# Attention: the out-projection directly behind P·V, its maximum pairs at other places, tile 14's maxima rounded in two halves

## Chip, cores and metric

The kernel runs on one core of a Trainium2 chip. The metric is device time in microseconds (us) of that core, lower is better. A step of the profile is read by the engines' short names: PE is TensorE (PEld its weight loads), DVE VectorE, ACT ScalarE, POOL GpSimd, SP SyncE.

## The reference

The program is two rounds of a Fourier layer and an attention layer with one shared K/V head, each with a residual, on x of shape 1 x 2048 x 512. There are 32 heads of width 16.

```python
x = x + _A_ref(_layernorm(x), ...)     # y = Cr@a - Ci@b,  a, b = x @ Wd_re.T, x @ Wd_im.T
x = x + _B_ref(_layernorm(x), wq, wk, wv, wo)
# the same two lines once more

def _B_ref(x, wq, wk, wv, wo):
    q = heads(x @ wq);  k = x @ wk;  v = x @ wv
    scores = jnp.einsum("bhqd,bkd->bhqk", q, k) * (Dh ** -0.5)
    p = _softmax(scores, axis=-1)
    o = jnp.einsum("bhqk,bkd->bhqd", p, v)
    return merge_heads(o) @ wo
```

The change touches only the attention layer (`_B_ref`), which runs twice, as layer 0 and layer 1.

## The kernel before

Each layer has a phase A (Fourier layer, Q, K, V) and a phase B (attention). Phase B goes through 16 query tiles of 128 rows. A tile `i` takes 32 steps `s_`: two halves of the heads by 16 key blocks of 128 keys. The order of all instructions is written by hand; each engine runs its own in that order and waits on semaphores.

In a step of `phase_b` TensorE does three things. First `pv` (L787): P·V of the step two before, eight matmul passes that write columns of bank `z`. Then `score` (L773): four score matmuls, 64 rows deep, so that two run beside each other in the two halves of the array; two of them fill a `pair()` of banks `x`, of which there are two, and ScalarE takes the exponential of a pair at once (L776). Between the scores stand up to three maxima: `max_half` (L350) computes the scores of a later tile against 512 keys into one of three banks `y`, and VectorE reduces them to a maximum per row (L351). These maxima are needed before a tile's own scores, since the softmax subtracts them: `max_neg` negates and rounds them into a high and a low part, and `max_rows` transposes them (L379), copies them (L381) and sends them by four DMAs of SyncE into the rows of the query tile that the score matmul adds. For most tiles this is done at steps 27 and 29 of the tile before. For tile 0 and tile 15 it is done in two halves: the first there (for tile 0 ahead of attention), the second at steps 11 and 13 of the tile itself.

The maxima are a list `units`, in order of tile, head pair, key quarter and half `g`. `owed(n)` lets three go in a step, after a lead of 12 ahead of attention, and `more_max` takes the next. The head pair has two maxima, one for each half of the array; when both are issued together they run side by side (a pair of maxima, below).

The tile's result goes out in the steps of the next tile (`out_tasks`): store, sums, reciprocal and load in steps 1 to 6, scaling (L827) and splitting (L833, L834) on GpSimd in steps 9 and 10. At the end of step 12 stands `o_proj`: twelve full-size matmuls (L86 to L88) that accumulate into one bank `y`, with a pair of maxima behind the sixth and the twelfth; `o_add` (L852) adds the residual on VectorE and issues the DMA of the result (L853), on GpSimd's queue in layer 0 and SyncE's in layer 1. So the projection of tile `i - 1` stands in the steps of tile `i`; 14 tiles of each layer (0 to 13) have pairs in it, tile 14's stands where no maxima are left, and tile 15's is done behind the steps.

Once all maxima are done, in tile 15, the last two scores of a step go to banks `y` of their own (L766), each with its own exponential (L768).

Of the kernel before, what the change touches and what calls it, by code (L numbers as in the profile page):

```python
# [17 lines left out]
P = 128  # L18
# [22 lines left out]
KEPT = [e for e in EARLY if e[0]]  # L41
QSLOT = (8, 0, 1, "h", "l", 8, 0, 1, "h", "l", 8, 0, 1, 8, 0, 1)
HALF = NPAIR // 2


@with_exitstack
def fnet_mqa_kernel(ctx: ExitStack, tc: tile.TileContext, x_in, ct, dt_, wq, wkv, wo, out):
# [50 lines left out]
    nc.gpsimd.memset(v1[:, :, DH:DH + 1], 1.0)  # L98
    kone = sb.tile([P, 1], F32, name="kone")
    kmask = sb.tile([P, 1], F32, name="kmask")  # L100
    t_ = sb.tile([P, 1], F32, name="ktmp")
    nc.vector.tensor_reduce(kone[:64], ident[:64, M0:M0 + 2], op=ALU.add, axis=AX.X)
    nc.vector.tensor_reduce(kone[64:], ident[64:, 64 + M0:64 + M0 + 2], op=ALU.add, axis=AX.X)
    nc.vector.tensor_reduce(t_[:64], ident[:64, M0:64], op=ALU.add, axis=AX.X)
# [82 lines left out]
    def make_layer(L, src, mid, dst, last):  # L187
# [176 lines left out]
        def max_neg(i, p0=0, n=NPAIR, k=4):  # L364
            nm = sb.tile([P, NPAIR, 2], F32, name="nm")[:, :n, :]
            nc.vector.tensor_reduce(nm, o.mxp[i][:, p0:p0 + n, :, :k], op=ALU.max, axis=AX.X, negate=True)
            if p0 + n == NPAIR:
                o.mxp.pop(i)
            nmv = nm.rearrange("p a g -> p g a")
            ms = sb.tile([P, 2, 2, NPAIR], F32, name="ms").rearrange("p g r a -> p (g r a)")  # L370
            ms = ms[:, :4 * n].rearrange("p (g r a) -> p g r a", g=2, r=2)
            nc.vector.tensor_copy(ms[:, :, 0, :].bitcast(F32R), nmv)
            nc.vector.tensor_sub(ms[:, :, 1, :].bitcast(F32R), nmv, ms[:, :, 0, :])
            st["ms"] = ms
# [160 lines left out]
        def phase_a(extra):  # L535
# [193 lines left out]
                if g == 0:  # L729
                    v_tr(12, 4, vt[0])  # L730
            max_neg(0, 0, HALF, 5)
            for k in range(12):
                more_max()
                if k == 2:
                    max_rows(0, 0, HALF, nc.scalar)

        early = {e[:2] for e in EARLY}
        units = [(0, pr, g, 3) for pr in range(HALF, NPAIR) for g in range(2)]
        units += [(i, pr, g, kb) for i in range(1, NT) for pr in range(NPAIR) for kb in range(4) for g in range(2)
                  if (i, kb) not in early]  # L740
        o.done = o.extra = 0

        def more_max():
            if o.done < len(units) and units[o.done][0] in o.loaded | {0}:
                max_half(*units[o.done])
                o.done += 1

        def owed(n):
            return min(3 * (n + 1) + 12 + o.extra, len(units)) - o.done

        def done_with(i, pr):
            return all(u[:2] > (i, pr) for u in units[o.done:])

        ptiles = {}

        def score(i, s_, j):
            hf, c = divmod(s_, NT)
            jj, g = divmod(j, 2)
            cp = 4 * (2 * hf + jj)
            if (i, s_) not in ptiles:  # L760
                k = i * NSTEP + s_
                ptiles[i, s_] = slot((6, 7, 2)[k % 3]).rearrange("p (j n) -> p j n", j=4)
            w = j // 2
            if i == NT - 1 and jj == 1 and o.done == len(units):
                e = bank("y")
                nc.tensor.matmul(e, kz[64 * g:64 * g + KR, c * P:(c + 1) * P],  # L766
                                 o.qT[i][64 * g:64 * g + KR, cp:cp + 4, :], start=True, stop=True)
                nc.scalar.activation(ptiles[i, s_][:, j, :], e, AF.Exp, scale=DH ** -0.5)  # L768
                return
            first = "e" not in st  # L770
            if first:
                st["e"] = pair()
            nc.tensor.matmul(st["e"][:, g, :], kz[64 * g:64 * g + KR, c * P:(c + 1) * P],  # L773
                             o.qT[i][64 * g:64 * g + KR, cp:cp + 4, :], start=True, stop=True)
            if not first:
                nc.scalar.activation(ptiles[i, s_][:, 2 * w:2 * w + 2, :], st.pop("e"), AF.Exp, scale=DH ** -0.5)  # L776
# [48 lines left out]
        def o_scale(i, hf):  # L825
            cs = slice(hf * 256, hf * 256 + 256)
            nc.gpsimd.tensor_mul(bt["ot"][:, cs], bt["ot"][:, cs], bt["den"][:, cs])  # L827
# [14 lines left out]
        def o_proj(i):  # L842
            for k in range(NK):
                o_mm(k)
                if k % 2 and i < NT - 1:
                    for _ in range(2):
                        more_max()
                        o.extra += 1
            o_add(i)

        def o_add(i):
            nc.vector.tensor_add(bt["x"], bt["po"], bt["x"])  # L852
            (nc.sync if last else nc.gpsimd).dma_start(dst[i], bt["x"])  # L853

        def finish():
            i = NT - 1
            oa = acc.pop((i, 1))
            x_load(i)
            pt = bank("y")
            for b in range(4):  # L860
                nc.tensor.transpose(pt[:, b * P:(b + 1) * P], oa[:, b * P:(b + 1) * P], ident)
            o_mm(0)
            o_mm(1)
            p4 = pt.rearrange("p (b j r) -> p b j r", b=4, j=4)
            rc = sb.tile([P, 4, 4], F32, name="rc")
            nc.vector.reciprocal(rc, p4[:, :, :, DH])
            on = half(5)[:, :256]
            for jj in range(2):
                nc.vector.tensor_tensor(
                    on[:, jj * P:(jj + 1) * P].rearrange("p (b g d) -> p b g d", b=4, g=2),  # L870
                    p4[:, :, 2 * jj:2 * jj + 2, :DH],
                    rc[:, :, 2 * jj:2 * jj + 2].unsqueeze(3).to_broadcast([P, 4, 2, DH]), op=ALU.mult)
            pt = bank("y")[:, :256]
            for jj in range(2):
                nc.tensor.transpose(pt[:, jj * P:(jj + 1) * P], on[:, jj * P:(jj + 1) * P], ident)
            split_ps(pt, bt["oh"][:, 256:], bt["ol"][:, 256:])
            o_mm(2)
            o_mm(3)
            o_add(i)

        o.finish = finish

# [25 lines left out]
        def phase_b(nxt):  # L908
# [10 lines left out]
            for n in range(NT * NSTEP):  # L919
                i, s_ = divmod(n, NSTEP)  # L920
                if len(behind) == 2:
                    pv(*behind.pop(0))
                behind.append((i, s_))
                g = units[o.done][2] if o.done < len(units) else 1
                for j, m in ((1 - g, 1), (g, 2), (3 - g, 0), (2 + g, 1)):
                    score(i, s_, j)
                    for _ in range(m):
                        if owed(n) >= 1:
                            more_max()
                if i == 0 and 2 <= s_ <= 8 and s_ % 2 == 0:  # L930
                    q_half_store(14, s_ // 2 - 1)
                if n == 12:
                    osp = slot(3, F32R).rearrange("p (a h n) -> p a h n", a=2, h=2)
                if i == 0 and s_ in (12, 14, 16, 18):
                    j = s_ // 2 - 6
                    split_sb(st["wo", j], woh[:, j, :], wol[:, j, :], nc.gpsimd)
                if i > 0:
                    for fn in out_tasks(i - 1).get(s_, ()):
                        fn()
                if s_ == 2:  # L940
                    for j in range(2, NT):
                        if i == max(0, j - 4 if j < 13 else j - 2):
                            qT_load(j)
                for fn in half_tasks(i).get(s_, ()):
                    fn()
                for at, j, p0, np_ in ((NT - AHEAD, i, HALF, HALF), (NSTEP - AHEAD, i + 1, 0, HALF if i == NT - 2 else NPAIR)):
                    if j in (0, NT - 1) or j == i + 1 < NT:
                        if s_ == at:
                            assert done_with(j, p0 + np_ - 1)
                            max_neg(j, p0, np_)  # L950
                        if s_ == at + 2:
                            max_rows(j, p0, np_)
# [6 lines left out]
        def half_tasks(i):  # L959
            return {  # L960
                18: [lambda: o_store(i, 0)], 19: [lambda: o_sum(i, 0)], 22: [lambda: o_inv(i, 0)],
                23: [lambda: o_load(i, 0)], 27: [lambda: o_scale(i, 0)], 29: [lambda: o_hi(i, 0)],
            }

        def out_tasks(i):
            return {
                1: [lambda: o_store(i, 1), lambda: o_sum(i, 1), lambda: x_load(i)], 5: [lambda: o_inv(i, 1)],
                6: [lambda: o_load(i, 1)], 9: [lambda: o_scale(i, 1)], 10: [lambda: o_hi(i, 1)],
                12: [lambda: o_proj(i)], 14: [lambda: o_stats(i)], 16: [lambda: o_rstd(i)],
                25: [lambda: o_ln(i)], 26: [lambda: o_xnh(i)], 27: [lambda: o_xnl(i)],  # L970
            }

        woh = wol = osp = None
# [48 lines left out]
```

## Time and profile before

| | us |
|---|---|
| three runs: median (lowest to highest) | 3716.96 (3715.03 to 3717.65) |
| the profiled execution: its time | 3724.12 |
| its span, first to last instruction | 3722.3 |
| attention of layer 0, about | 690 to 1865 |
| attention of layer 1, about | 2541 to 3713 |

The times of attention are those of the first and last P·V matmuls in the trace. The granted TensorE clock is 1.00 in attention and 0.99 over the span. In the views a row of the timeline gives the start (us from the span's start), the duration, the engine, the line, the operation with its output and inputs, the number of instructions merged, and in brackets the idle time before them with the releaser. Two rows of one engine can overlap, since matmuls and vector operations are pipelined.

### The profile page before, as it was taken

What the parts mean: (1) busy time and instruction counts of PE and PEld (TensorE: products, weight loads), DVE (VectorE), ACT (ScalarE), POOL (GpSimd) and SP (SyncE); (2) the same over time, 40 slices, a digit from 0 to 9 for tenths busy, and PEclk for the clock granted to TensorE, in tenths of its full rate; (3) what the DMA queues carried; (4) which work ended last, traced back from release to release, by engine and by line L of the source; (5) the groups of instructions that cost most, each with busy time, mean ns of one, the idle gap of its engine ahead of it and who ended that gap; (6) DMA issues with size and microseconds to landing.
All of it is one profiled execution on the core that took longest, in us unless ns stands there. A gap on an engine that the chain in (4) does not pass through costs nothing. (4 is left out here: it accounts for less than half of the span.)

```text
span 3722.3 us, 64512 instructions
## 1 busy us (share of the span) xinstructions
PE 3631.1 (98%) x25474; PEld 1909.3 (51%) x25474; DVE 2798.4 (75%) x4767; ACT 2400.3 (64%) x3104; POOL 777.3 (21%) x984
## 2 busy tenths in 40 slices
PE   8999999999999999999999999999999999999999
PEld 6786768533433333334377766684343334333333
DVE  5167978788888888888311779778888888888882
ACT  4322222688888888888933231227888888888888
POOL 5534332111111111111154342421000000000000
PEclk9999999999999999999999999999999999999999
DMA  5444241311111100110143342313111111001100
GB/s 176 133 136 125 97 119 52 101 32 50 33 36 31 49 22 24 33 47 23 40 131 104 129 124 92 110 64 89 47 33 36 33 49 34 22 22 50 33 24 25
DMA packets 204736, 243.00 MB, mean 65 GB/s; under 512 B 36880, under 2 KB 160784, under 8 KB 197264
## 3 DMA queue, kind: packets, MB, share of 16 engines
q1 hardware_dynamic: 199504, 222.08, 20.1%
q0 software_dynamic: 4864, 16.78, 1.5%
q8 instruction: 199, 3.26, 0.4%
q14 instruction: 105, 0.86, 0.1%
q10 hardware_dynamic: 64, 0.02, 0.0%
HBM read 174.58 MB, written 63.17 MB: 64 GB/s over the span
## 5 line engine op out<-in xcount | busy, mean ns | idle before, releaser
L776 ACT ACTIVATE slot<-x 128x1024 f32<-128x1024 f32 x1990 | 1943.1, 1027 | 334.4 <-PE x L773 265.5
L351 DVE TENSOR_REDUCE mxp<-y 128x1 f32<-128x512 f32 x3040 | 1908.1, 684 | 281.5 <-PE y L350 233.3
L787 PE MATMUL z<-slot,v 128*32 128x512 f32 x8192 | 1096.3, 605 | 1.9 <-ACT row L790 1.9
L773 PE MATMUL x<-slot,kz 64*128 64x512 f32 x2956 | 900.9, 447 | 3.6 <-DMA slot<-mt 3.5
L773 PEld LDWEIGHTS x<-slot,kz 64*128 64x128 f32 x2956 | 375.3, 185 | 731.5 <-ACT slot L776 598.5
L350 PE MATMUL y<-kz,slot 64*128 64x512 f32 x2208 | 726.2, 435 | 4.8 <-ACT mt L381 0.7
L338 DVE TENSOR_REDUCE mxe<-y 128x1 f32<-128x512 f32 x832 | 516.4, 682 | 189.4 <-PE y L336 184.7
L660 PE MATMUL x<-ch,xnh 64*128 64x512 f32 (+1 forms) x2048 | 507.8, 390 | 16.3 <-DVE slot L74 8.9
L660 PE MATMUL x<-ch,xnl 64*128 64x512 f32 (+1 forms) x2048 | 475.2, 369 | 0.0
L660 PE MATMUL x<-cl,xnh 64*128 64x512 f32 (+1 forms) x2048 | 474.7, 369 | 0.0
L350 PEld LDWEIGHTS y<-kz,slot 64*128 64x128 f32 x2208 | 349.5, 185 | 94.5 <-DVE mxp L351 27.5
L827 POOL TENSOR_TENSOR row<-row,row 128x256 f32<-128x256 f32 x63 | 46.3, 735 | 1677.8 <-DMA row<-rd 1422.6
L336 PE MATMUL y<-kz,slot 64*128 64x512 f32 (+1 forms) x1088 | 354.3, 420 | 33.7 <-DVE mxe L338 20.7
L78 POOL TENSOR_TENSOR cl<-craw,ch 128x512 fp32r<-128x512 f32 x236 | 303.1, 1303 | 289.2 <-ACT ch L77 229.3
L787 PEld LDWEIGHTS z<-slot,v 128*32 128x32 f32 x8192 | 163.6, 108 | 277.3 <-issue 249.2
L660 PEld LDWEIGHTS x<-ch,xnh 64*128 64x128 f32 x2048 | 268.7, 189 | 69.2 <-issue 16.4
L660 PEld LDWEIGHTS x<-ch,xnl 64*128 64x128 f32 x2048 | 280.7, 189 | 33.3
L660 PEld LDWEIGHTS x<-cl,xnh 64*128 64x128 f32 x2048 | 281.7, 190 | 28.0
L77 ACT CAST ch<-craw 128x512 fp32r<-128x512 f32 x256 | 154.8, 620 | 161.8 <-PE x L660 89.5
L666 ACT COPY junk<-x 128x2 f32<-128x2 f32 x256 | 40.5, 158 | 332.3 <-PE x L660 253.6
L336 PEld LDWEIGHTS y<-kz,slot 64*128 64x128 f32 x1088 | 171.8, 188 | 129.4 <-DVE mxe L338 90.5
L338 DVE TENSOR_REDUCE mxp<-y 128x1 f32<-128x512 f32 (+1 forms) x256 | 144.4, 617 | 24.7 <-PE y L336 21.5
(148 smaller groups left out, 3141.7 us busy)
## 6 DMA issues: line engine op xcount, KB each, us to landing
craw<-ct_in SPq DMA_DIRECT2D x112, 512.0 KB
slot<-qd SPq DMA_DIRECT2D x44, 1024.0 KB
qd<-row SPq DMA_DIRECT2D x144, 128.0 KB
od<-row SPq DMA_DIRECT2D x252, 64.0 KB
row<-x_in SPq DMA_DIRECT2D x32, 256.0 KB
mid<-row POOLq DMA_DIRECT2D x32, 256.0 KB, 2.4
craw<-ct_in SPq DMA_DIRECT2D x32, 256.0 KB
row<-mid SPq DMA_DIRECT2D x32, 256.0 KB
```

The lines of the kernel that those rows point to most:

```text
L77: nc.scalar.copy(hi, raw)
L78: (eng or nc.vector).tensor_sub(lo, raw, f(hi))
L336: nc.tensor.matmul(pm[g], o.qT[i][gs, pr, :], kz[gs, c0:c0 + n], start=True, stop=True)
L338: nc.vector.reduce_max(to[:, g:g + 1], pm[g], axis=AX.X)
L350: nc.tensor.matmul(pm, o.qT[i][gs, pr, :], kz[gs, kb * 512:kb * 512 + 512], start=True, stop=True)
L351: nc.vector.reduce_max(partial(i)[:, pr, g, kb:kb + 1], pm, axis=AX.X)
L660: nc.tensor.matmul(z[d][:, cols], w, hl[j][t == 1][rs_], start=m == 0 and ph == 0 and j == t == 0, stop=j == 1 and t == 2 and (ph == 0 or ...
L666: nc.scalar.copy(junk, zp[dd][:, :, cols.start])
L773: nc.tensor.matmul(st["e"][:, g, :], kz[64 * g:64 * g + KR, c * P:(c + 1) * P], o.qT[i][64 * g:64 * g + KR, cp:cp + 4, :], start=True, sto ...
L776: nc.scalar.activation(ptiles[i, s_][:, 2 * w:2 * w + 2, :], st.pop("e"), AF.Exp, scale=DH ** -0.5)
L787: nc.tensor.matmul(a[32 * j:32 * j + 32, :], v1[:, c, :], pt[:, j, :], start=c == 0, stop=c == NT - 1)
L827: nc.gpsimd.tensor_mul(bt["ot"][:, cs], bt["ot"][:, cs], bt["den"][:, cs])
```

## The change

Five things change in phase B; nothing else does, apart from two small tiles that are dropped (`ms` and `ktmp` use other buffers).

- `o_proj(i - 1)` stands directly behind the P·V of step 12, ahead of that step's scores, not at the step's end.
- Its pairs of maxima stand behind the third and the ninth matmul, and for tiles 9 to 13 also behind the sixth.
- Step 11 has two maxima (no `odd` one). All other steps have two of one pair (`whole`) and one half of another (`odd`), whose other half is taken in the next step.
- Tile 14 is rounded in two halves, as tile 15 is: `HALVED`.
- The DMA of the result is issued by SyncE in both layers, in step 13 (`o_out`); scaling and splitting on GpSimd stand together in steps 28 and 10.

```diff
+HALVED = (0, NT - 2, NT - 1)
...
-            ms = sb.tile([P, 2, 2, NPAIR], F32, name="ms").rearrange("p g r a -> p (g r a)")
-            ms = ms[:, :4 * n].rearrange("p (g r a) -> p g r a", g=2, r=2)
+            ms = half(0 if i or p0 else 2)[:, :4 * n].rearrange("p (g r a) -> p g r a", g=2, r=2)
...
-            for k in range(12):
-                more_max()
-                if k == 2:
+            for k in range(6):
+                max_both(*pick_pair(0))
+                if k == 1:
                     max_rows(0, 0, HALF, nc.scalar)
...
+        def pick_odd(n):
+            if "odd" in st:
+                return *st.pop("odd"), 1
+            pick = pick_pair(n, n + 1)
+            if pick:
+                st["odd"] = pick
+                return *pick, 0
+            return None
+
+        def max_both(j, pr, kb):
+            for g in range(2):
+                max_half(j, pr, g, kb)
...
         def o_proj(i):
             for k in range(NK):
                 o_mm(k)
-                if k % 2 and i < NT - 1:
-                    for _ in range(2):
-                        more_max()
-                        o.extra += 1
+                if (k in (0, 2) or k == 1 and 8 < i) and i < NT - 1:
+                    pick = pick_pair(NSTEP * (i + 1) + 12)
+                    if pick:
+                        max_both(*pick)
             o_add(i)
...
-            (nc.sync if last else nc.gpsimd).dma_start(dst[i], bt["x"])
+
+        def o_out(i):
+            nc.sync.dma_start(dst[i], bt["x"])
...
                 behind.append((i, s_))
-                g = units[o.done][2] if o.done < len(units) else 1
-                for j, m in ((1 - g, 1), (g, 2), (3 - g, 0), (2 + g, 1)):
-                    score(i, s_, j)
-                    for _ in range(m):
-                        if owed(n) >= 1:
-                            more_max()
+                if i > 0 and s_ == 12:
+                    o_proj(i - 1)
+                whole = pick_pair(n)
+                odd = pick_odd(n) if i == 0 or s_ != 11 else None
+                g = odd[3] if odd else 1
+                score(i, s_, 1 - g)
+                if whole:
+                    max_half(*whole[:2], g, whole[2])
+                score(i, s_, g)
+                if whole:
+                    max_half(*whole[:2], 1 - g, whole[2])
+                if odd:
+                    max_half(*odd[:2], g, odd[2])
+                score(i, s_, 3 - g)
+                score(i, s_, 2 + g)
...
-                    if j in (0, NT - 1) or j == i + 1 < NT:
+                    if j in HALVED or j == i + 1 < NT:
...
-                23: [lambda: o_load(i, 0)], 27: [lambda: o_scale(i, 0)], 29: [lambda: o_hi(i, 0)],
+                23: [lambda: o_load(i, 0)], 28: [lambda: o_scale(i, 0), lambda: o_hi(i, 0)],
...
-                6: [lambda: o_load(i, 1)], 9: [lambda: o_scale(i, 1)], 10: [lambda: o_hi(i, 1)],
-                12: [lambda: o_proj(i)], 14: [lambda: o_stats(i)], 16: [lambda: o_rstd(i)],
+                6: [lambda: o_load(i, 1)], 10: [lambda: o_scale(i, 1), lambda: o_hi(i, 1)],
+                12: [lambda: o_proj(i)] if i == NT - 1 else [],
+                13: [lambda: o_out(i)], 14: [lambda: o_stats(i)], 16: [lambda: o_rstd(i)],
```

`pick_pair` takes the next head pair and key quarter whose query tile is loaded, in the same order as `units` had them. The lines of the code shift: P·V is L815 after, the scores L801, the maxima L351 with their reduction in L352, the projection L87 to L89, the addition L880.

What TensorE has in step 12 of tile 4 in layer 0, from its last two scores to the P·V of step 13 (`slot_9653` is the query tile of the maxima, `slot_8282` the weights of the projection), before:

```order
L773 MATMUL x<-xnl,kz 128x512 x2
L86 MATMUL y<-slot_7957,slot_8282 128x512
L87 MATMUL y<-slot_7958,slot_8282 128x512
L88 MATMUL y<-slot_7957,slot_8282 128x512
L86 MATMUL y<-slot_7957,slot_8282 128x512
L87 MATMUL y<-slot_7958,slot_8282 128x512
L88 MATMUL y<-slot_7957,slot_8282 128x512
L350 MATMUL y<-kz,slot_9653 128x512 x2
```

The same six matmuls and one more pair follow, and then P·V. After, from the P·V of step 12 on:

```order
L815 MATMUL z<-slot_11449,v_74 32x512 x4
L87 MATMUL y<-slot_7956,slot_8281 128x512
L88 MATMUL y<-slot_7957,slot_8281 128x512
L89 MATMUL y<-slot_7956,slot_8281 128x512
L351 MATMUL y<-kz,slot_9649 128x512 x2
```

and at the end of the same projection, with the scores and maxima of step 12 behind it:

```order
L351 MATMUL y<-kz,slot_9649 128x512 x2
L87 MATMUL y<-slot_7956,slot_8281 128x512
L88 MATMUL y<-slot_7957,slot_8281 128x512
L89 MATMUL y<-slot_7956,slot_8281 128x512
L801 MATMUL x<-xnl,kz 128x512
L351 MATMUL y<-kz,slot_9649 128x512
L801 MATMUL x<-xnl,kz 128x512
L351 MATMUL y<-kz,slot_9649 128x512 x2
L801 MATMUL x<-xnl,kz 128x512 x2
```

The scores have moved from ahead of the projection to behind it, and its last pair has moved from its end to three matmuls ahead of its end; the bank of the projection is now asked for again by the third maximum of the same step.

The projection of tile 9 (step 12 of tile 10, layer 0), after, from its first to its third pair:

```order
L351 MATMUL y<-kz,slot_14540 128x512 x2
L87 MATMUL y<-slot_7956,slot_8281 128x512
L88 MATMUL y<-slot_7957,slot_8281 128x512
L89 MATMUL y<-slot_7956,slot_8281 128x512
L351 MATMUL y<-kz,slot_14540 128x512 x2
L87 MATMUL y<-slot_7956,slot_8281 128x512
L88 MATMUL y<-slot_7957,slot_8281 128x512
L89 MATMUL y<-slot_7956,slot_8281 128x512
L351 MATMUL y<-kz,slot_14540 128x512 x2
```

Here a pair stands behind every third matmul; before, the two pairs of every projection were six matmuls apart.

The last maxima, in tile 15 of either layer, stand in step 3 before and in steps 3, 4 and (one of them) 5 after.

More of the change, by code (lines that the diff above doesn't have):

```diff
@@ L100, in fnet_mqa_kernel @@
     kmask = sb.tile([P, 1], F32, name="kmask")
-    t_ = sb.tile([P, 1], F32, name="ktmp")
+    t_ = junk[:, :1]
     nc.vector.tensor_reduce(kone[:64], ident[:64, M0:M0 + 2], op=ALU.add, axis=AX.X)
@@ L731, in phase_a @@
             max_neg(0, 0, HALF, 5)
-            for k in range(12):
-                more_max()
-                if k == 2:
+            for k in range(6):
+                max_both(*pick_pair(0))
+                if k == 1:
                     max_rows(0, 0, HALF, nc.scalar)
         early = {e[:2] for e in EARLY}
-        units = [(0, pr, g, 3) for pr in range(HALF, NPAIR) for g in range(2)]
-        units += [(i, pr, g, kb) for i in range(1, NT) for pr in range(NPAIR) for kb in range(4) for g in range(2)
-                  if (i, kb) not in early]
@@ L741, in make_layer @@
[L741 to L749, printed above, removed]
-        def done_with(i, pr):
-            return all(u[:2] > (i, pr) for u in units[o.done:])
+        groups = {}
+        for i in range(NT):
+            for hf in range(2) if i in HALVED else (None,):
+                prs = range(NPAIR) if hf is None else range(HALF * hf, HALF * hf + HALF)
+                if i or hf:
+                    kbs = [kb for kb in range(4) if (i, kb) not in early] if i else [3]
+                    at = NSTEP * i + NT - AHEAD if hf else NSTEP * (i - 1) + NSTEP - AHEAD
+                    groups[i, hf] = {"at": at, "whole": [(pr, kb) for pr in prs for kb in kbs]}
@@ new lines, in in_reach, with pick_pair @@
+        def in_reach(j, n):
+            return j in o.loaded | {0} and (j <= 1 or n >= NSTEP * max(0, j - 4 if j < 13 else j - 2) + 8)
+        def pick_pair(n, until=0):
+            for (j, _), g in groups.items():
+                if not in_reach(j, n):
+                    return None
+                if g["at"] < until:
+                    continue
+                if g["whole"]:
+                    pr, kb = g["whole"].pop(0)
+                    return j, pr, kb
+            return None
@@ new lines, in pick_odd @@
+        def pick_odd(n):
[5 more added lines that the diff above has]
+                return *pick, 0
+            return None
+        def max_both(j, pr, kb):
+            for g in range(2):
+                max_half(j, pr, g, kb)
+        def done_with(i, pr):
+            if "odd" in st and st["odd"][0] <= i and st["odd"][1] <= pr:
+                return False
+            return not any(q <= pr for (j, _), g in groups.items() if j <= i for q, *_ in g["whole"])
@@ L754, in make_layer, with all_done @@
+        def all_done():
+            return not any(g["whole"] for g in groups.values()) and "odd" not in st
         ptiles = {}
@@ L763, in score @@
             w = j // 2
-            if i == NT - 1 and jj == 1 and o.done == len(units):
+            if i == NT - 1 and jj == 1 and all_done():
                 e = bank("y")
@@ L879, in finish @@
             o_add(i)
+            o_out(i)
         o.finish = finish
@@ L945, in phase_b @@
                     fn()
-                for at, j, p0, np_ in ((NT - AHEAD, i, HALF, HALF), (NSTEP - AHEAD, i + 1, 0, HALF if i == NT - 2 else NPAIR)):
-                    if j in (0, NT - 1) or j == i + 1 < NT:
+                for at, j, p0, np_ in ((NT - AHEAD, i, HALF, HALF),
+                                       (NSTEP - AHEAD, i + 1, 0, HALF if i + 1 in HALVED else NPAIR)):
+                    if j in HALVED or j == i + 1 < NT:
                         if s_ == at:
-                            assert done_with(j, p0 + np_ - 1)
+                            assert done_with(j, p0 + np_ - 1), (n, j, p0, groups)
                             max_neg(j, p0, np_)
@@ L967, in out_tasks @@
                 1: [lambda: o_store(i, 1), lambda: o_sum(i, 1), lambda: x_load(i)], 5: [lambda: o_inv(i, 1)],
-                6: [lambda: o_load(i, 1)], 9: [lambda: o_scale(i, 1)], 10: [lambda: o_hi(i, 1)],
-                12: [lambda: o_proj(i)], 14: [lambda: o_stats(i)], 16: [lambda: o_rstd(i)],
-                25: [lambda: o_ln(i)], 26: [lambda: o_xnh(i)], 27: [lambda: o_xnl(i)],
+                6: [lambda: o_load(i, 1)], 10: [lambda: o_scale(i, 1), lambda: o_hi(i, 1)],
+                12: [lambda: o_proj(i)] if i == NT - 1 else [],
+                13: [lambda: o_out(i)], 14: [lambda: o_stats(i)], 16: [lambda: o_rstd(i)],
+                25: [lambda: o_ln(i), lambda: o_xnh(i)], 26: [lambda: o_xnl(i)],
             }
```

## The prediction

> **What bounds the kernel now.** I read the busy shares first, then a window that holds only attention (its columns are TensorE, its weight loads, VectorE, ScalarE and GpSimd), then the timeline of single steps.
>
> ```profile
> PE 3631.1 (98%) x25474; PEld 1909.3 (51%) x25474; DVE 2798.4 (75%) x4767; ACT 2400.3 (64%) x3104; POOL 777.3 (21%) x984
> ```
>
> ```profile
> 800.00:1800.00 1000.00, 993.50 (x6730) 392.96 (x6722) 880.80 (x1505) 855.72 (x910) 147.65 (x312) 1.00 0.12 33
> ```
>
> The averages say TensorE (98%), and inside attention TensorE has 99%, VectorE 88% and ScalarE 86% (880.80 and 855.72 us of 1000). A matmul counts as busy while it drains, so 99% does not show that TensorE sets the pace. For that one ordinary step is read: TensorE, then the sum of its weight loads' waits for a score bank (us, times, longest), then ScalarE.
>
> ```profile
> 1006.06 1.07 PE L787 MATMUL z<-slot,v 128*32 128x512 f32 x8
> 1007.05 0.50 PE L773 MATMUL x<-xnl,kz 64*128 64x512 f32 x1
> 1007.06 0.72 PE L350 MATMUL y<-kz,slot 64*128 64x512 f32 x2
> 1007.39 0.39 PE L773 MATMUL x<-xnl,kz 64*128 64x512 f32 x1
> 1007.62 0.39 PE L350 MATMUL y<-kz,slot 64*128 64x512 f32 x1
> 1007.75 0.50 PE L773 MATMUL x<-xnl,kz 64*128 64x512 f32 x2
> 1008.18 1.06 PE L787 MATMUL z<-slot,v 128*32 128x512 f32 x8
> ```
>
> ```profile
> PEld x L773 <- ACT slot L776: 812.0, 1007, 1.8
> ```
>
> ```profile
> 1005.76 1.94 ACT L776 ACTIVATE slot<-x 128x1024 f32<-128x1024 f32 x2 [0.18 <-PE x L773]
> ```
>
> A step lasts 1008.18 - 1006.06 = 2.12 us, P\*V start to P\*V start. The two exponentials end at 1005.76 + 1.94 = 1007.70, and the third score starts at 1007.75: it waits for a score bank. Back the other way, ScalarE waits 0.18 us for the second score. So a step is a ring of TensorE and ScalarE over two score buffers; the third maximum (1007.62) stands in the gap in front of the third score and costs next to nothing there. That matters below.
>
> **The out-projection before.** TensorE, the two loads that wait, VectorE:
>
> ```profile
> 1010.58 0.47 PE L86 MATMUL y<-slot,slot 128*128 128x512 f32 x1 [0.21 <-DVE mxp L351]
> ...
> 1011.79 0.39 PE L88 MATMUL y<-slot,slot 128*128 128x512 f32 x1
> 1012.11 0.49 PE L350 MATMUL y<-kz,slot 64*128 64x512 f32 x2
> 1012.54 0.50 PE L86 MATMUL y<-slot,slot 128*128 128x512 f32 x1
> 1012.87 0.40 PE L87 MATMUL y<-slot,slot 128*128 128x512 f32 x1
> 1013.11 0.39 PE L88 MATMUL y<-slot,slot 128*128 128x512 f32 x1
> ...
> 1013.80 0.39 PE L88 MATMUL y<-slot,slot 128*128 128x512 f32 x1
> 1014.12 0.49 PE L350 MATMUL y<-kz,slot 64*128 64x512 f32 x2
> 1014.54 1.07 PE L787 MATMUL z<-slot,v 128*32 128x512 f32 x8
> 1015.54 0.49 PE L773 MATMUL x<-xnl,kz 64*128 64x512 f32 x1
> ...
> 1017.25 1.06 PE L787 MATMUL z<-slot,v 128*32 128x512 f32 x8
> ```
>
> ```profile
> 1015.99 0.18 PEld L350 LDWEIGHTS y<-kz,slot 64*128 64x128 f32 x1 [0.15 <-DVE mxp L351]
> 1016.59 0.18 PEld L350 LDWEIGHTS y<-kz,slot 64*128 64x128 f32 x1 [0.42 <-DVE row L852]
> ```
>
> ```profile
> 1012.64 1.29 DVE L351 TENSOR_REDUCE mxp<-y 128x1 f32<-128x512 f32 x2 [1.01 <-PE y L350]
> 1014.65 1.29 DVE L351 TENSOR_REDUCE mxp<-y 128x1 f32<-128x512 f32 x2 [0.72 <-PE y L350]
> 1015.85 0.68 DVE L852 TENSOR_TENSOR row<-y,row 128x512 f32<-128x512 f32 x1
> ```
>
> Count from the P\*V of step 12 (1008.18). The next two P\*V start at 1014.54 and 1017.25, so the two steps take 9.07 us where 4.24 is usual. Two stalls are in it: 0.21 us in front for one of three y banks, and about 0.6 us in the step behind, where the second and third maximum wait for banks that the pair and the addition (L852) still hold. The change removes the first stall for certain. The question is what happens to the second.
>
> Intervals that I reuse: P\*V to the next matmul 1.00 (1014.54 to 1015.54); three projection matmuls after a pair 0.57 to the third (1012.54 to 1013.11), three more 0.69 (to 1013.80); matmul to pair 0.32 (1011.79 to 1012.11); pair to matmul 0.42 (1014.12 to 1014.54 has the same); second score 0.34 behind the first (1007.05 to 1007.39). VectorE starts 0.53 behind a pair (1012.11 to 1012.64), takes 0.60 from start to start (two from 1014.65 to 1015.85), lasts 0.68, and its bank is taken again 0.06 us after its end (15.25 + 0.68 against 15.99).
>
> **1. All 28 out-projections, with two pairs.** Zero is the P\*V of step 12. Projection at 1.00, first pair at 1.00 + 0.57 + 0.32 = 1.89, second pair at 1.89 + 0.42 + 0.57 + 0.69 + 0.32 = 3.89, first score at 3.89 + 0.42 + 0.57 + 0.32 = 5.20. VectorE: the second pair's maxima start at 4.42 and 5.02, the addition at 5.62; banks come free at 5.16, 5.76 and 5.62 + 0.68 + 0.06 = 6.36. So the step's first maximum (5.20) finds its bank, the second waits until 5.76, the third until 6.36, and the scores queued behind it wait with it. P\*V follows 0.66 behind that maximum, as 1016.59 to 1017.25 did: 7.02. The next step is ordinary, 2.12, and ends at 9.14 against 9.07. The front stall is gone, but the rear one has grown, because the last pair is now only three matmuls ahead of the scores instead of one whole P\*V. **+0.07 us each, +2 in all.** The change from P\*V's shape to the projection's is not in these rows; I take P\*V to scores (1.00) and leave 0.1 us either way, 2.8 in the sum.
>
> **2. The step with two maxima** (step 11, 28 times). Its third score still waits for ScalarE (1007.70 to 1007.75), so I take 0. The gain's other end is one matmul's 0.23 us (0.69 / 3), 6.4 in the sum; a loss has no reason, since nothing is added there.
>
> **3. A third pair for tiles 9 to 13 of each layer (10).** Put a pair at 0. Its banks come free at 0.53 + 0.68 + 0.06 = 1.27 and at 1.87. The next pair, three matmuls on, is due at 0.42 + 0.57 + 0.32 = 1.31: its first half goes, its second half waits 0.56 us, and the projection queued behind it on TensorE waits too. Only two banks are there, the third holds the sum of the projection. The pair after that is then due at 1.87 + 1.31 = 3.18, where its banks are back. Without the extra pair it would be 2.00. **+1.18 each, +11.8 in all.** Ends: 0.62 without the wait, 1.74 if the last pair waits as well, so 5.6 either way. In a step these maxima cost almost nothing, as shown.
>
> A rule speaks against the change here. The Trainium skill, "TensorEngine Tiling (Array Packing)", section "Tiling Modes", says that changing the tiling mode, not merely the tile, drains TensorE. The trace agrees: 0.32 us where the mode changes, 0.23 where it doesn't. By the rule each extra pair between projection matmuls pays twice, and inside a step it pays nothing; the sum stays as it is, since those gaps are in the intervals.
>
> **4. Tile 14 in two halves.** One more transpose, here that of step 29 of tile 4:
>
> ```profile
> 1049.47 1.07 PE L787 MATMUL z<-slot,v 128*32 128x512 f32 x8
> ...
> 1051.82 0.30 PE L379 MATMUL y<-ident,ms 128*64 128x128 f32 x1
> 1052.05 1.07 PE L787 MATMUL z<-slot,v 128*32 128x512 f32 x8
> ```
>
> 2.58 against 2.12: +0.46 per layer, +0.9. The rows have the same three steps to land as here. If they came late, say by 0.4 us, it would be 0.8 more; below 0.9 nothing, as the other transpose stays.
>
> **5. The end of the maxima.** Before, they end in step 3 of tile 15, after in step 5.
>
> ```profile
> 3649.87 1.07 PE L787 MATMUL z<-slot,v 128*32 128x512 f32 x8
> ...
> 3653.20 1.06 PE L787 MATMUL z<-slot,v 128*32 128x512 f32 x8
> ...
> 3656.79 0.68 PE L787 MATMUL z<-slot,v 128*32 128x512 f32 x4
> ```
>
> Step 3 took 3.33 us, steps 4 and 5 together 3.59, so 1.80 each; all three 6.92. After, steps 3 and 4 are ordinary (4.24), and step 5, with one maximum, lies between 1.80 and 3.33; with fewer banks in use I take 2.2, near the first. That is 6.44: -0.5 per layer, -1.0 (ends -1.8 and +1.3).
>
> **6. At nothing.** The projection's operands are needed about 1.4 us earlier and the GpSimd work moves a step:
>
> ```profile
> 1003.34 0.75 POOL L834 TENSOR_TENSOR slot<-row,slot 128x256 fp32r<-128x256 f32 x1
> ```
>
> They are ready at 1003.34 + 0.75 = 1004.09 and wanted at 1008.18 + 1.00 = 1009.18, which leaves 5 us; it would cost from there on. The result's DMA moves from GpSimd's queue (layer 0) to SyncE's, a step later, with the next store five steps on. Tile 14's projection, in tile 15's steps (two in all), keeps its twelve matmuls and has no pair: 0, 0.3 either way. The row buffer that now holds the rounded maxima was stored many steps before, and the twelve maxima ahead of attention are as many as before.
>
> **Sum:** 2 + 0 + 11.8 + 0.9 - 1.0 = +13.7 us, on the profiled execution's 3724.12 us: 3737.8. That execution is 7.16 us over the median of the three runs, 3716.96; from the median it is **3730.7**.
>
> **The rivals.** *Shorter steps and free banks:* the third pair never waits (-5.6) and step 11 loses a matmul (-6.4): +1.7, 3718.7, no change; either alone gives about 3725. For it: TensorE is busy 99%. Against: the third score's wait for ScalarE, and two banks for maxima that take 0.60 each.
> *Faster:* no bank is ever late at the projection, neither behind it nor between its pairs. P\*V would then start as in an ordinary step, 1.13 behind the first score (1007.05 to 1008.18) instead of 1.82, 0.69 x 28 = 19.3 us less, and the third pairs 5.6 less: -11.2, 3705.8. It decides at the addition: the third maximum asks at 5.20 + 1007.62 - 1007.05 = 5.77, so the addition must have given its bank back by then and not at 6.36. For it: VectorE has a full P\*V to empty its queue before the projection. Against: both maxima of the last pair stand ahead of the addition.
> That the projection is not moved is no rival: the order shows it.
>
> **How the numbers follow.** Forecast 0.60 (own range 3725 to 3740: the unknowns 2.8, 5.6 and about 2 in part together), no change 0.24, faster 0.16. The range reaches down into the second case, 3712, and up to 3740, leaving out the fast case and a little above. A measurement of this kernel tells about 0.2% (7.4 us) from no change: faster 0.17, same 0.23, slower 0.60.
>
> **What would show it.** Right: step 12 of a two-pair tile about 7.0 us, the step behind it 2.12; a tile with three pairs 1.2 us longer, with a wait for a maximum (L352) in front of the second half of its second pair; step 11 still 2.12. Wrong: step 11 near 1.9, a step 12 near 6.3, or projection operands that arrive late.

## The result and the profile after

The changed kernel takes 3738.13 us (median of 4 runs, 3735.79 to 3741.99), the kernel before beside it 3717.31 (3715.03 to 3719.70). The ratio is 1.0057, with an interval of 1.0040 to 1.0074: slower by 15 to 28 us. 3730.7 was predicted. The profiled executions took 3738.62 and 3724.12 us, 14.5 us apart, against a sum of +13.7 made on that execution.

The page's first line and the window that holds only attention, after:

```profile
PE 3647.1 (98%) x25476; PEld 1905.9 (51%) x25476; DVE 2801.1 (75%) x4773; ACT 2400.8 (64%) x3102; POOL 766.2 (21%) x968
```

```profile
800.00:1800.00 1000.00, 994.25 (x6666) 388.07 (x6664) 872.08 (x1493) 847.84 (x900) 139.35 (x299) 1.00 0.12 33
```

Nothing shows at this height: TensorE is as busy as before, and VectorE and ScalarE do about 1% less in the same 1000 us, because the steps are longer. The steps have to be read. Here is step 12 of tile 4 in layer 0, whose order the change section shows: TensorE's P·V and the pairs, then the two loads of maxima that wait for a bank, then VectorE.

```profile
1006.83 1.07 PE L815 MATMUL z<-slot,v 128*32 128x512 f32 x8
...
1008.96 1.07 PE L815 MATMUL z<-slot,v 128*32 128x512 f32 x8
1009.95 0.50 PE L87 MATMUL y<-slot,slot 128*128 128x512 f32 x1
...
1010.85 0.49 PE L351 MATMUL y<-kz,slot 64*128 64x512 f32 x2
...
1012.86 0.49 PE L351 MATMUL y<-kz,slot 64*128 64x512 f32 x2
...
1014.18 0.49 PE L801 MATMUL x<-xnl,kz 64*128 64x512 f32 x1
...
1015.99 1.07 PE L815 MATMUL z<-slot,v 128*32 128x512 f32 x8
```

```profile
1014.74 0.18 PEld L351 LDWEIGHTS y<-kz,slot 64*128 64x128 f32 x1 [0.26 <-DVE mxp L352]
1015.34 0.18 PEld L351 LDWEIGHTS y<-kz,slot 64*128 64x128 f32 x1 [0.42 <-DVE row L880]
```

```profile
1013.39 1.29 DVE L352 TENSOR_REDUCE mxp<-y 128x1 f32<-128x512 f32 x2 [0.73 <-PE y L351]
1014.60 0.68 DVE L880 TENSOR_TENSOR row<-y,row 128x512 f32<-128x512 f32 x1
```

Measured from the P·V at 1008.96: projection 0.99, pairs 1.89 and 3.90, first score 5.22, second maximum 5.78, third 6.38, next P·V 7.03. The prediction had 1.00, 1.89, 3.89, 5.20, 5.76, 6.36 and 7.02. The wait in front of the projection is gone; the wait for the addition (`row L880`) is there again, in the same step now.

The step of tile 10 in layer 0 has a third pair. Its second pair is the place:

```profile
1455.31 0.49 PE L351 MATMUL y<-kz,slot 64*128 64x512 f32 x2
...
1456.63 1.05 PE L351 MATMUL y<-kz,slot 64*128 64x512 f32 x2
...
1458.50 0.51 PE L351 MATMUL y<-kz,slot 64*128 64x512 f32 x2
```

```profile
1456.62 0.18 PEld L351 LDWEIGHTS y<-kz,slot 64*128 64x128 f32 x1 [0.36 <-DVE mxp L352]
1457.18 0.18 PEld L351 LDWEIGHTS y<-kz,slot 64*128 64x128 f32 x1 [0.37 <-DVE mxp L352]
```

The second pair takes 1.05 us where the first and the third take 0.49 and 0.51, because its two halves no longer run side by side: the second is loaded at 1457.18, 1.87 us behind the first pair, when VectorE returns a bank. The third pair then starts 3.19 us behind the first.

The time from one step's P·V to the next, summed over both layers from the P·V rows of the two traces (us):

| steps | before | after | difference | predicted |
|---|---|---|---|---|
| 12 and 13 of tiles 1 to 9 (18 projections, two pairs) | 163.61 | 164.89 | +1.3 | +1.3 |
| 12 and 13 of tiles 10 to 13 (8, three pairs) | 72.75 | 82.68 | +9.9 | +10.0 |
| 12 to 18 of tile 14 (2, three pairs, and the halves) | 40.03 | 44.09 | +4.1 | +3.4 |
| 11 of tiles 1 to 14 | 59.79 | 59.24 | -0.5 | 0 |
| 0 to 31 of tile 15 | 134.52 | 132.37 | -2.1 | -1.0 |
| 29 of tiles 0 to 14 | 76.98 | 78.77 | +1.8 | 0 |
| 0 of tiles 1 to 14 | 62.72 | 64.33 | +1.6 | 0 |
| all steps of attention | 2340.95 | 2356.92 | +16.0 | +13.7 |

The projections with a third pair carry the loss. Each row of "predicted" is worked out from the terms on record (0.07 and 1.18 per projection, 0.46 per layer for the halves). What remains is small and spread. The -0.5 of step 11 is two single steps (2.40 us in tile 5 of layer 1 before, 1.90 in tile 13 of layer 0 after); all others took 2.11 to 2.14 in both. Step 0 varies from trace to trace: in tile 11 of layer 0 it took 3.13 us before, 3.85 after and 2.12 in the first experiment, because its first score starts late.

### The profile page after: what moved, and what is told of

Same layout as the page of the kernel before. It is cut to its first block, busy times and chain, and to the rows that moved or that the text cites. A ratio compares the mean times of both kernels' runs of the same rounds, so it can differ in the third digit from the quotient of the medians.

```text
span 3736.8 us, 64654 instructions
## 1 busy us (share of the span) xinstructions
PE 3647.1 (98%) x25476; PEld 1905.9 (51%) x25476; DVE 2801.1 (75%) x4773; ACT 2400.8 (64%) x3102; POOL 766.2 (21%) x968
## 5 line engine op out<-in xcount | busy, mean ns | idle before, releaser
L352 DVE TENSOR_REDUCE mxp<-y 128x1 f32<-128x512 f32 x3040 | 1909.8, 684 | 302.2 <-PE y L351 238.5
L815 PE MATMUL z<-slot,v 128*32 128x512 f32 x8192 | 1096.1, 605 | 1.9 <-ACT row L818 1.9
L801 PE MATMUL x<-slot,kz 64*128 64x512 f32 x2964 | 903.1, 447 | 6.0 <-DMA slot<-mt 3.1
L801 PEld LDWEIGHTS x<-slot,kz 64*128 64x128 f32 x2964 | 377.3, 185 | 729.8 <-ACT slot L804 591.4
L351 PE MATMUL y<-kz,slot 64*128 64x512 f32 x2208 | 733.0, 436 | 6.4 <-DVE mxp L352 1.5
L351 PEld LDWEIGHTS y<-kz,slot 64*128 64x128 f32 x2208 | 349.9, 185 | 103.8 <-DVE mxp L352 38.7
L815 PEld LDWEIGHTS z<-slot,v 128*32 128x32 f32 x8192 | 163.4, 108 | 276.9 <-issue 248.6
```

The lines of the kernel that those rows point to most:

```text
L351: nc.tensor.matmul(pm, o.qT[i][gs, pr, :], kz[gs, kb * 512:kb * 512 + 512], start=True, stop=True)
L352: nc.vector.reduce_max(partial(i)[:, pr, g, kb:kb + 1], pm, axis=AX.X)
L815: nc.tensor.matmul(a[32 * j:32 * j + 32, :], v1[:, c, :], pt[:, j, :], start=c == 0, stop=c == NT - 1)
```

## The experiments

All are compared with the kernel before on the same chip (its median lay between 3716.66 and 3719.51). The medians carry some us of noise, so step times of the traces are given beside them. Most of that noise goes with the granted clock of an execution: among the 55 runs of the kernel before that stand beside the experiments, the 7 at a mean clock of 0.992 took 3721.7 us on average and the 25 at 0.994 took 3717.1. In the traces it lies outside attention, whose clock is 1.00: what is not attention, the same work in all these kernels but for details, took 1373.8 to 1382.5 us.

**Without the third pairs.**

```diff
-                if (k in (0, 2) or k == 1 and 8 < i) and i < NT - 1:
+                if k in (0, 2) and i < NT - 1:
```

> The changed kernel without its third pairs (tiles 9 to 13 of each layer). Theory, the third pairs are the loss: step 12 of tiles 10 to 14 falls from 8.21 to 7.04 us, 11.7 us in ten projections; the maxima end three steps later in tile 15, which gives back about 1.3 us; so about 10.4 us under the changed kernel, and 0.1 to 0.3% over the kernel before. Rival, the third pairs pay for themselves in the steps they empty: within 3 us of the changed kernel.

3725.02 us, ratio 1.0016 (1.0007 to 1.0025). Step 12 of tiles 10 to 14 takes 7.03 to 7.05 us, against 8.20 to 8.24 with the third pair. Its P·V rows for tile 10 in layer 0:

```profile
1453.45 1.06 PE L815 MATMUL z<-slot,v 128*32 128x512 f32 x8
...
1460.50 1.06 PE L815 MATMUL z<-slot,v 128*32 128x512 f32 x8
```

Between the two traces attention is 11.3 us shorter: 11.8 less in those ten steps, 2.9 more in tile 15, where the maxima end in step 8, and 1.9 less in step 0 of layer 0, most of it tile 11's late first score. That tile 15 gives back 2.9 and not 1.3 was not foreseen; the third pairs do pay for part of themselves there, but a quarter. They are the loss.

**The third maximum back in step 11**, on top of that:

```diff
-                odd = pick_odd(n) if i == 0 or s_ != 11 else None
+                odd = pick_odd(n)
```

> e1 with the third maximum back in step 11. Theory, that maximum stands in the gap in front of the third score: step 11 stays at 2.11 to 2.12 us, and the time falls by about 1 us against e1, since the maxima end sooner. Rival, TensorE's matmuls set the step: step 11 grows by 0.1 to 0.23 us, 3 to 6 us over e1.

3723.72 us, 1.0011 (1.0003 to 1.0020). Step 11 keeps its length:

```profile
1004.45 1.06 PE L815 MATMUL z<-slot,v 128*32 128x512 f32 x8
...
1006.03 0.40 PE L351 MATMUL y<-kz,slot 64*128 64x512 f32 x1
1006.14 0.52 PE L801 MATMUL x<-xnl,kz 64*128 64x512 f32 x2
1006.59 1.06 PE L815 MATMUL z<-slot,v 128*32 128x512 f32 x8
```

1006.59 - 1004.45 = 2.14, and 1008.96 - 1006.83 = 2.13 in the changed kernel without that maximum. Tile 15 is 1.0 us shorter in the two layers together. Leaving one of three maxima out of an ordinary step buys nothing, as predicted. One step differs: in tile 13 of layer 0 step 11 took 1.90 us with two maxima in the changed kernel and in the first experiment, and 2.13 with three here. ScalarE's exponentials started early there (the third score waited 0.19 us for them, where 0.41 is usual with two maxima), so a maximum is free only as long as ScalarE is the later one.

**The projection in its old place**, on top of the first experiment: the move alone undone.

```diff
-                if i > 0 and s_ == 12:
-                    o_proj(i - 1)
                 whole = pick_pair(n)
...
                 score(i, s_, 2 + g)
+                if i > 0 and s_ == 12:
+                    o_proj(i - 1)
...
-                if (k in (0, 2) or k == 1 and 8 < i) and i < NT - 1:
+                if k in (1, 3) and i < NT - 1:
```

> e1 with the projection back behind the scores of step 12 and its two pairs behind the sixth and the twelfth matmul: the move alone undone. Theory, the move is neutral because its rear stall grew by what the front one saved: steps 12 and 13 take 6.38 + 2.70 = 9.08 instead of 7.04 + 2.12 = 9.16, 2 us under e1. Rivals: the move itself is the loss (5 us or more under e1), or it is a gain that the third pairs hid (5 us or more over e1).

3719.69 us, 1.0001 (0.9992 to 1.0010). In tiles 1 to 13 steps 12 and 13 take 6.37 to 6.42 and 2.69 to 2.71, together 9.10, against 9.16 in the first experiment; attention is 2.4 us shorter. The medians are 5.3 us apart, with intervals that overlap; at the two clocks with most runs they lie 2.0 us (0.994: 2 and 5 runs) and 2.9 us (0.992: 4 and 2 runs) apart, which agrees with the traces. The move by itself is no gain, and by the traces a loss of 2 to 3 us.

**The two-maximum step at 12 instead of 11**, on top of the first experiment:

```diff
-                odd = pick_odd(n) if i == 0 or s_ != 11 else None
+                odd = pick_odd(n) if i == 0 or s_ != 12 else None
```

> e1 with the two-maximum step at 12 instead of 11, so that no maximum asks for the projection's bank in that step. Theory, the wait for that bank is the rear stall: step 12 falls from 7.04 to about 6.4 us with step 13 at 2.12, 28 times, 16 to 18 us under e1 and 0.2 to 0.4% under the kernel before. Rival, ScalarE's idle time or the changes of the array's tiling hold the scores behind the projection: step 12 stays at 7.0.

3705.09 us, 0.9967 (0.9956 to 0.9978), faster than both kernels. The step behind the projection, from its first score to the next P·V, and its only load that still waits:

```profile
1011.09 0.50 PE L801 MATMUL x<-xnl,kz 64*128 64x512 f32 x1
1011.09 0.50 PE L351 MATMUL y<-kz,slot 64*128 64x512 f32 x1
1011.43 0.39 PE L801 MATMUL x<-xnl,kz 64*128 64x512 f32 x1
1011.64 0.49 PE L351 MATMUL y<-kz,slot 64*128 64x512 f32 x1
1011.66 0.71 PE L801 MATMUL x<-xnl,kz 64*128 64x512 f32 x2
1012.30 1.06 PE L815 MATMUL z<-slot,v 128*32 128x512 f32 x8
```

```profile
1011.64 0.18 PEld L351 LDWEIGHTS y<-kz,slot 64*128 64x128 f32 x1 [0.26 <-DVE mxp L352]
```

P·V follows the first score after 1.21 us, where the changed kernel had 1015.99 - 1014.18 = 1.81. Nothing asks for the projection's bank any more in that step, and step 12 takes 6.42 to 6.46 us instead of 7.04. Attention is 16.3 us shorter than in the first experiment. ScalarE and the changes of tiling were the same in both, so they do not hold this step. Run again beside the kernel of the last experiment, it took 3706.09 us, 0.9965 (0.9952 to 0.9979):

> e4 once more, beside e8 on one chip. Theory: step 12 at 6.44 and step 13 at 2.12 again, within 3 us of e8 and 0.3 to 0.4% under the kernel before.

**Tile 14 in halves, alone**, on the kernel before:

```diff
-                for at, j, p0, np_ in (..., (NSTEP - AHEAD, i + 1, 0, HALF if i == NT - 2 else NPAIR)):
-                    if j in (0, NT - 1) or j == i + 1 < NT:
+                for at, j, p0, np_ in (..., (NSTEP - AHEAD, i + 1, 0, HALF if i in (NT - 3, NT - 2) else NPAIR)):
+                    if j in (0, NT - 2, NT - 1) or j == i + 1 < NT:
```

> The kernel before with nothing but tile 14 rounded in two halves. Theory: one more transpose in step 13 of tile 14, +0.4 to 0.5 us per layer, and up to 0.8 us in step 16 where the rows land late; about 1 to 2 us in all, no change by the median. Rival, the second half's rows are late in both layers: step 16 over 3 us in each.

3719.01 us, 0.9999 (0.9990 to 1.0008). Steps 12 and 13 of tile 14 take 6.61 to 6.62 and 2.92 to 2.93, each 0.2 longer, so 0.42 to 0.44 per layer. The size is as expected, but only the half in step 13 is the transpose; in step 12 the projection's first matmul waits 0.42 us for a bank instead of 0.20, behind the three small operations that round the maxima on VectorE. Step 16 did not change in either layer. In the changed kernel it did: step 16 of tile 14 takes 3.05 us in layer 0, 2.52 before, and 2.19 and 2.12 in layer 1. The last of the four DMAs of the rows is issued there at 1770.17 and the first score, due about 1771.6, starts at 1772.57. The trace does not record when the rows landed, so that they were late is inferred. The projection's place alone does not decide it: with the projection in its old place step 16 took 2.51 us in the third experiment and 3.33 in the last one.

**One pair only**, behind the third matmul, with three maxima in every step (tiles 0 and 1 keep two pairs, so that the maxima end in time):

```diff
-                if (k in (0, 2) or k == 1 and 8 < i) and i < NT - 1:
+                if (k == 0 or k == 2 and i < 2) and i < NT - 1:
...
-                odd = pick_odd(n) if i == 0 or s_ != 11 else None
+                odd = pick_odd(n)
```

> The projection behind P*V with one pair only, behind its third matmul (tiles 0 and 1 keep two), and three maxima in steps 11 and 12; the maxima end in step 11 of tile 15. Theory, worked out as in the prediction: first score 4.58 us behind the P*V, addition's bank back at 5.49, asked for at 5.15, so step 12 takes 6.15 us; against e4 (6.44) 26 times 0.29 = 7.5 us less, 1.4 us given back in tile 15: about 6 us under e4. Rival, the bank that the projection holds is asked for as late as with two pairs: step 12 at 6.4 or more, and no gain over e4.

3705.91 us, 0.9968 (0.9956 to 0.9981): as fast as the two-maximum step, not 6 us faster. The step was as expected:

```profile
1011.52 0.18 PEld L801 LDWEIGHTS x<-xnl,kz 64*128 64x128 f32 x1 [0.35 <-issue]
...
1012.43 0.18 PEld L351 LDWEIGHTS y<-kz,slot 64*128 64x128 f32 x1 [0.61 <-DVE row L880]
...
1013.09 0.16 PEld L815 LDWEIGHTS z<-slot,v 128*32 128x32 f32 x8 [0.36 <-issue]
```

The third maximum still waits for the addition, 0.91 us behind the first score and not 1.16, and step 12 takes 6.08 to 6.17 us. That is 0.32 less than with two maxima there, in 24 projections (not 26), 7.6 us. It was lost again in three places: tile 15 takes 3.0 us more, not 1.4, since the maxima end in its step 11; the four projections that keep two pairs are back at 7.05 (+0.6 each, 2.4), which the expectation had left out; and in this trace step 0 took 2.4 us more in all.

**One maximum instead of the third pair's two:**

```diff
-                if (k in (0, 2) or k == 1 and 8 < i) and i < NT - 1:
+                if k in (0, 2) and i < NT - 1:
                     pick = pick_pair(NSTEP * (i + 1) + 12)
                     if pick:
                         max_both(*pick)
+                elif k == 1 and 8 < i < NT - 1:
+                    odd = pick_odd(NSTEP * (i + 1) + 12)
+                    if odd:
+                        max_half(*odd[:2], odd[3], odd[2])
```

> The changed kernel with one maximum instead of a pair behind the sixth matmul of tiles 9 to 13. It still changes the array's tiling twice, but its bank is back in time. Theory, 1.17 us of a third pair are 0.62 for the changes of tiling and the matmul itself and 0.56 for the bank: step 12 of those tiles at 7.66 us. Rivals: all of it is the tiling (8.2), or all of it is the bank (7.05 to 7.3).

3731.60 us, 1.0031 (1.0018 to 1.0043), and step 12 of those tiles takes 7.65 to 7.68 us, as expected. In tile 10 of layer 0, between the two pairs:

```profile
1457.80 0.50 PE L351 MATMUL y<-kz,slot 64*128 64x512 f32 x2
...
1459.11 0.50 PE L351 MATMUL y<-kz,slot 64*128 64x512 f32 x1
1459.55 0.50 PE L87 MATMUL y<-slot,slot 128*128 128x512 f32 x1
...
1460.44 0.50 PE L351 MATMUL y<-kz,slot 64*128 64x512 f32 x2
```

The single maximum starts 1.31 us behind the first pair, without a wait, and the next pair 2.64 behind it. So the third pair's 1.17 us are 0.62 for the gaps around it with its own matmul, and 0.55 for the bank.

**The two-maximum step behind the projection in its old place**: the third experiment with that step at 13.

```diff
-                odd = pick_odd(n) if i == 0 or s_ != 11 else None
+                odd = pick_odd(n) if i == 0 or s_ != 13 else None
```

> e3 (projection in its old place, two pairs) with the two-maximum step at 13 instead of 11, the step behind the projection there. Theory, the place of the projection matters little and the third maximum behind it is what costs: step 13 falls from 2.70 to 2.12 us, 28 times, about 16 us under e3 and the kernel before, the same as e4 within 3 us. Rival, the gain of e4 needs the move: within 5 us of e3.

3704.04 us, 0.9968 (0.9956 to 0.9980). From the step behind the projection to the one after:

```profile
1015.84 1.06 PE L815 MATMUL z<-slot,v 128*32 128x512 f32 x8
...
1017.94 1.06 PE L815 MATMUL z<-slot,v 128*32 128x512 f32 x8
```

Step 13 takes 2.10 us here instead of 2.70, and 2.09 to 2.11 in all of tiles 1 to 13; the kernel is as fast as with the projection behind P·V. So the gain does not need the move; it needs that no third maximum asks for the projection's bank.

## Why the prediction was right

- *What sets a step.* A step was read as a ring of TensorE and ScalarE, with the third maximum in a gap. Step 11 kept 2.12 us with two maxima and with three, in 27 of its 28 places. The rival in which TensorE's matmuls set the step is out but for one step; the gap holds the third maximum and no more.
- *The move, +0.07 each.* Measured +1.3 in 18 projections, 0.07 each. Undoing it alone brought 2.4 us of attention. The prediction put this to the wait behind, which grew as the one in front went. The rows show that as a part only. Against an ordinary step the part behind the projection is 0.59 us longer before (1017.25 - 1014.54 = 2.71, against 2.12) and 0.68 after (1.81 from first score to P·V, against 1.13), so it took back 0.09. The rest is the projection's own stretch, 4.23 us from its first matmul to the next score where it was 3.96 to the next P·V; what stood in front was 0.28 (2.40 from P·V to the first matmul, against 2.12), 0.21 of it the wait. That the wait behind is the third maximum's, at the bank of the addition, is shown by the two experiments that keep that maximum away: 14 to 16 us of attention, which both kernels lose there.
- *The fast rival* asked that the addition be done by 5.77. Its bank came at 6.38, and its wait was real; the changed kernel does nothing about it. With one maximum less in that step and no third pairs the time is 3705.09, beside that rival's 3705.8; that they meet is partly chance, since the rival counted 0.69 us a step and the experiment gained 0.60.
- *The third pair, +1.18 each.* Measured 1.17, split as on record: 0.62 without the wait, the rest the second bank. The last pair did not wait, so the upper end (1.74) fell.
- *The price of a pair among projections.* Of the 1.17 us, 0.62 are the matmul with the gaps on both sides of it, and 0.55 a bank. The clock had no part in it: it was granted at 1.00 in the window above. The Trainium skill, "TensorEngine Tiling (Array Packing)", section "Tiling Modes", says that a change of mode drains TensorE. The trace agrees in the 0.62: 0.32 us from a projection matmul to a pair and 0.42 from a pair to the next, where projection matmuls follow each other every 0.23. The rest of the loss is not of this kind.
- *Tile 14,* +0.9: the size is right, with 0.42 to 0.44 per layer on the kernel before, but it was laid to the transpose alone. The row that it was read from, step 29, also holds a wait for VectorE; the transpose itself is 0.23 us ahead of P·V. In the changed kernel step 16 of layer 0 is 0.5 us longer as well, which the prediction had as an upper end (rows that land late, here inferred).
- *The end of the maxima,* -1.0: mis-sized, -2.0 in steps 3 to 6 and -2.1 in all of tile 15. Step 5 with its one maximum took 1.89 us, where 2.2 was taken between 1.80 and 3.33, and step 6 took 1.69 where it was 1.89 before.
- *At nothing:* right for the projection's operands, which no wait names. Step 29 was left out, and it is +1.8 in all, from 2.57 to 2.63 us in most tiles. The transpose did not change (it waits 0.37 us for a bank, 0.36 before, and P·V follows it by 0.23 in both); in the rows of tile 6, layer 0, the third maximum gets its bank 1.74 us behind P·V instead of 1.69. One thing that changed stands neither in the list of changes nor in the prediction: in layer 0 two of the GpSimd operations of the next layer's norm moved one step earlier, within steps 25 to 27. Steps 25 to 28 together differ by 0.05 us over tiles 1 to 14 of that layer.
- *The size.* The time is 7 us over the 3730.7 and near the upper end of the range. The profile's +14.5 and attention's +16.0 lie by the sum of +13.7; the medians' 20.8 is more, and its interval, from 15 to 28, leaves the 13.7 out. The clock accounts for some of it, by an estimate: the changed kernel's two runs at 0.992 took 3737.64 and 3738.62 us, 16 to 17 over the 3721.7 of the kernel before at that clock, though not in runs beside each other. Against attention's +16.0 the sum is 2.3 us short: tile 14 and steps 0 and 29 took more, tile 15 less. The rest of the medians' difference stays open.

## What to carry to other kernels

Where a small ring of PSUM banks feeds a vector engine, count for each request which release it takes, in order: a long accumulation that holds one bank puts a wait wherever the next request for that bank stands, and moving the accumulation alone bought nothing here. Take the request away for one step instead; here one maximum less, in the right step, was worth 14 to 16 us of attention (0.4%), and in the step before it nothing. Work that fills a gap for free in one stage can cost full price in another: the third maximum of an ordinary step cost nothing, and a third pair inside the projection 1.2 us.

## What was not expected

The last step with maxima costs 3.33 us with three of them, 2.73 with two and 1.89 with one, since the scores that then go to banks `y` ask for the same banks: with three, the first of them waits 0.78 us for VectorE. So tile 15's steps 0 to 11 take 24.0 us in the changed kernel, whose 16 last maxima end on one, and 25.0 before, where 12 end on three. The steps 29 grew by 0.06 us in every kernel with the new order of maxima, also with the projection in its old place, and not in the one with tile 14 halved alone. Whether the order, the other buffer of the rounded maxima or the moved GpSimd work does it was not tried.
